# A linear-attention layer and a gated MLP on one Trainium2 core: one vector loaded by transfers, setup work on other engines, and a new table of zero matmuls

## The chip, the cores and the metric

The kernel runs on one core of a Trainium2 chip. The metric is device time in microseconds (us) of one execution; lower is better. Three runs of the kernel before gave 355.48, 359.37 and 359.94 us, median 359.37.

## What is computed

Inputs are float32. `r, k, v, w` are 4 x 8 x 768 x 48 (batch, head, token, channel); `u` is 8 x 48. The attention keeps a 48 x 48 state per head, and its output, laid out as 768 tokens of 384 channels, goes through a gated MLP that mixes along the tokens:

```python
for t in range(S):
    cur = np.einsum('bhd,bhe->bhde', u[None] * kt, vt)
    y[:, :, t] = np.einsum('bhd,bhde->bhe', rt, state + cur)
    state = wt[:, :, :, None] * state + np.einsum('bhd,bhe->bhde', kt, vt)
...
h = np.maximum(x @ w_in, 0.0)                       # 384 -> 1024
u, v = (h[..., :d_ff // 2], h[..., d_ff // 2:])
v_n = (v - mu) / np.sqrt(var + 1e-06)
v_s = np.einsum('ts,bsd->btd', w_spatial, v_n) + b_spatial[None, :, None]
gated = u * v_s
return (gated @ w_out).astype(np.float32)           # 512 -> 384
```

## The kernel before, in words

The work is cut into 24 slots (`NS`): 4 batches of 6 chunks of 128 tokens. A slot of the attention goes like this. `slot_load` fetches the decays `W`, the pair `kr` (k and r by channel) and `v`. `slot_prep` multiplies pairs of decays into `W2p`, scans them forward and back into `E` and `F`, and scales k and r with these. `slot_a` forms the 64 x 64 score tiles in PSUM (`paw`), and VectorE copies their lower half into a tile `AS` (two such tiles in turn, which must hold zeros elsewhere). `slot_kt` transposes k (`pt`, copied to `KT`), `slot_d` multiplies `KT` with `v` into `paw`, `slot_s` and `slot_w` carry the state `S0`, `S1`. `slot_y` and `slot_inter` accumulate the outputs in two PSUM banks, `PY[0]` and `PY[1]` (`py`), and `slot_x` adds the banks into `y`, transposes it (`yt`) and splits it into a high and a low part `xT`.

In the first six slots (`B_PE`) the term with `u` is a matmul: `rk` = r times k, then `pg` = `rk` times `up_sb`, where `up_sb` holds `u` by channel, one column per head (`bonus`, L445). VectorE multiplies `pg` with `v` into `bv`, and a matmul with the identity adds that to `PY[0]` (L597). `up_sb` is made in the kernel: `u_sb[:1]` is loaded as one row, eight matmuls (`spread`, L1112) turn it into columns in PSUM (`pu_`), and two copies (L1118) bring them to `up_sb`. Later slots multiply with the full `u_sb` and use `id64`, two 64 x 64 pieces of the identity.

The MLP follows slot by slot: `hv_unit` (`ph`), the mean and variance (`scale`), then per batch `g_unit` (`pu` for the gate, `pv` for the mix along the tokens) and `out_unit` (`po`, copied to `ot` and stored). Products of float32 are three fp32r matmuls of high and low parts (`mm3`, L714 to L716). The weights are fetched as raw 64-bit words and split by `split64`; the parts are called `wv`, `wu` and `wo`. `check_w` loads each decay tensor once more (`Nw`, L426) and tests it on ScalarE (L427); `Nw` shares one buffer with `N`.

The order of everything is written out by hand. Each operation is recorded with the engines that it may run on, and the table `PLAN` gives for each the engine (T for TensorE, V VectorE, A ScalarE, G GpSimd, S for SyncE, which issues the loads) and a start time; `plan` sorts by start, and each engine executes its operations in that order, waiting on semaphores. `place` gives tiles their buffers in the same order; the tag `pm` has three PSUM banks that `pg`, `pt`, `yt`, `ph`, `pu`, `pv` and `po` share.

Between real matmuls the kernel issues zero matmuls (`warm`, L1070): a 128 x 128 tile of zeros times itself, added to an unused part of the bank `PY[0]`. `fill` decides how many stand ahead of each TensorE operation: it walks through the planned times, and where it finds a gap of over 0.3 us, it puts in as many zeros as the gap should hold. It stops at the operation `last`, after slot 5. The first zeros wait for the clearing of `PY[0]` on VectorE.

The setup ahead of all that clears `zk`, `zz` and both banks `PY` on VectorE (L292 to L309), makes the identity on GpSimd, and copies `id64` (L326) and `mask` (L345) on VectorE. The two `AS` tiles are cleared in slots 0 and 1 by operations of the plan (L515), here on VectorE. `out_unit` stores a tile of 128 rows in one transfer, or in two where the condition with `SPLIT` holds (five tiles of batch 0).

Of the kernel before, what the change touches and what calls it, by code (L numbers as in the profile page):

```python
# [36 lines left out]
V47l A5e4 V5i8 S3o9 A3vo V4pz V4q2 V5cw A5k6 V5q2 S4gg V4jg V52c V52f V53t A5cy V5cz S4k4 V4xs V52e V52q V53u A5hd
V5ip T1xn T2eh T2gj A2ig A2ks A2lg Shm Swh Syv Gx6 T10u Vq1 V12b V139 Vqr Vsz Vt1 V13u G13y V1aw A1av A13x Vdv V16m
T1ax V1nv A175 T17h A19o T1js T1pc T1cb V1f0 A1fw V1tj T1tg A1ur V1ws T21r A23m T2b5 A2bs T2ii T2kd T2ma A2yd A2ye
A2z2 S1ca S1az S1dx V1c8 T1fy V1dw G1nu G1ez V1fz G1hq V1ik V1k8 G1nw V1th A1yy A1n3 V1iz T1vu V23n A1wf T1ny A1pa  # L40
T1zt T282 T1us V21t A21u V2ke T29g A2bv V2eg T2o8 A2p2 T2ry A2tr T2y8 T30j T32c A377 A378 A379 A3bl V39a V3iq G3t6
G3y9 G41y G41z V47o V4jf A4ji V4rz V4aj A4gi V4py A47p A4gj V5hc S1j1 S1j0 S2bz G2c1 T2c3 V2bw V2c5 G2q6 V2c4 V2d1
V2ef V2q7 G2p4 V2q8 A2gi A2yq V2ee T2st V3db A2nd T2p5 A2q4 T2q5 T3ha T2u5 V30i A3dc V3ei T3io A3lm V3m0 T3o7 A3vl
T3vm A40g T41w T45k T47h A4ag A4dx A4f5 S2yc S2ih S2y9 V2u6 T2vo V30f V39g V3fy V349 V3a4 V3ay V3d2 G3f7 G3oy A396
A3p0 V30h T3qv V3tk A3ph T3fz A3ip T3sn T3wf T3jz V3su A3vp V3we T3xs A47m V47q T49e V4dw T4fl A4gc T4k7 T4ma T4q4
A4ry A4xr A52b S3f8 S34b S3oa V35q T3li V3lj V3p1 V3oz V3lk V3o8 V3q6 V3qu G3qy G3tl A49g V40h V3vk T3z2 V4ah A47i
T3ul A3z4 T4a9 T4ch T40f V4ai G4cj T4dv V4ge V4gf T4jl V4o8 T4p4 A4pv T4s0 T4tx T4vt A4z8 A507 A52g A58b V570 V58g
V59y G5be G5dg V5e3 G5ha A5iq A5ju V5ol A5k7 A5k8 V5tz A5ln A5lo V5v2 T7x9 S3qx A41x S4ci A4dy S4jh A4xc S55k A5ec
T34a T35r T3bk A3ej T5n3 T5ok T5ri T5uh T5xc T5yt V60a V6lw A6oe V6z4 T376 T38n T3ow A3sw T5h9 T5it T5lp T5sy T60b
T61r V637 V6ge A6rs V6up T3a6 T3d1 T3ek A3gj T638 T665 T67l T692 T6aj T6bz V6ey V6fz A6xn V70k T443 T4gk T4hy A4je  # L50
T5ed T5fs T5k9 T5q1 T5vw T64o V6c5 G6t9 A7e9 G7ea T7lk T7n0 T7oh T80p A826 Sa8o T7fp T7h6 T7im T7k3 V7q3 S854 T7z8
T827 T83m T855 A86k Sdct T4xu T4z7 T5bf A5fu T6dg T6ex T6ha T6iz T6ur T6xm V70c G8cq A8kr G8lu T53v T55j T572 A5e5
T6kh T6nd T6ru T6t8 T6w7 T6z2 V7ct G7k7 A7wp V7wq T58h T59x T5cv A5is T7xm T86r T881 T89h T8ay T8cf V8hs G8ht A8j9
# [64 lines left out]
Tqnl Tqp1 Tqqh Tqry Aqtf Sqve Tqdb Tqj6 Tqkn Tqm3 Aqnk Sqtg Vof3 Tqth Vqua  # L118
"""

GAP, FILL_TO, COLD = 0.3, 5, 7.0

EARLY = 8

W3 = 5

KR, AB = 3, 2

SPLIT, PE_END = 5, 10

B_PE = 6

Q = 32
T = D - Q

# [1092 lines left out]
```

## Time and profile before

| | |
|---|---|
| median of three runs | 359.37 us (355.48 to 359.94) |
| the profiled execution | 357.4 us, of which the span from first to last instruction is 355.6 us |
| TensorE busy | 347.8 us, 98% |
| VectorE, ScalarE, GpSimd busy | 280.0, 223.8, 141.8 us |
| TensorE clock granted | 1.000 over the span |
| moved by DMA | 50.17 MB, 23,274 packets |

Busy time counts instructions from start to end; on TensorE neighbours overlap, and the zero matmuls count as busy too. One zero matmul is two rows of the trace, since a float32 matmul runs in two passes. Idle time of an engine is listed with what ended it. In a timeline a row merges equal instructions that follow each other: start, length from the first start to the last end, engine, line, operation, tiles, and count.

### The profile page before, as it was taken

What the parts mean: (1) busy time and instruction counts of PE and PEld (TensorE: products, weight loads), DVE (VectorE), ACT (ScalarE), POOL (GpSimd) and SP (SyncE); (2) the same over time, 40 slices, a digit from 0 to 9 for tenths busy, and PEclk for the clock granted to TensorE, in tenths of its full rate; (3) what the DMA queues carried; (4) which work ended last, traced back from release to release, by engine and by line L of the source; (5) the groups of instructions that cost most, each with busy time, mean ns of one, the idle gap of its engine ahead of it and who ended that gap; (6) DMA issues with size and microseconds to landing.
All of it is one profiled execution on the core that took longest, in us unless ns stands there. A gap on an engine that the chain in (4) does not pass through costs nothing.

```text
span 355.6 us, 11441 instructions
## 1 busy us (share of the span) xinstructions
PE 347.8 (98%) x4644; PEld 324.2 (91%) x4644; DVE 280.0 (79%) x626; ACT 223.8 (63%) x622; POOL 141.8 (40%) x187
## 2 busy tenths in 40 slices
PE   7999999989999999999999999999999999999998
PEld 6878887889999898799999999999999999899997
DVE  8988989898998856989787889676776486589750
ACT  2667989885646688896457646844163768464331
POOL 1242264013165436443546633753525217313630
DMA  7898548963256575653545545335020354230003
GB/s 217 229 269 253 173 145 250 257 192 111 72 150 182 148 205 173 190 142 98 156 133 169 162 147 169 101 111 166 23 90 25 98 182 115 64 113 0 24 25 113
DMA packets 23274, 50.17 MB, mean 141 GB/s; under 512 B 2737, under 2 KB 12082, under 8 KB 23218
## 3 DMA queue, kind: packets, MB, share of 16 engines
q1 hardware_dynamic: 23074, 49.21, 47.2%
q8 instruction: 37, 0.61, 0.8%
q14 instruction: 19, 0.16, 0.2%
q10 hardware_dynamic: 144, 0.20, 0.1%
HBM read 44.67 MB, written 4.72 MB: 139 GB/s over the span
## 4 chain that ended last, share of the span: by engine, by line
PE 82%; DMA 9%; DVE 4%; ACT 3%; issue 2%; POOL 0%; SPq 0%; DVEq 0%; POOLq 0%; ACTq 0%
PE pv L714 7%; PE pv L716 7%; PE pv L715 7%; PE py L587 5%; DMA Nw<-in_gt_dram 5%; PE po L714 4%; PE po L715 4%; PE po L716 4%; PE ph L714 4%; PE pu L714 4%; PE pu L716 4%; PE ph L716 4%; PE pu L715 4%; PE ph L715 4%; PE py L1070 3%; PE paw L551 3%
## 5 line engine op out<-in xcount | busy, mean ns | idle before, releaser
L714 PE MATMUL pv<-ws,vh 128*128 128x384 f32 x144 | 49.5, 344 | 1.1 <-ACT us L955 1.1
L716 PE MATMUL pv<-ws,vl 128*128 128x384 f32 x144 | 48.6, 338 | 0.0
L715 PE MATMUL pv<-ws,vh 128*128 128x384 f32 x144 | 48.5, 337 | 0.0
L714 PE MATMUL pu<-xT,wi 128*128 128x384 f32 x96 | 33.1, 345 | 0.3 <-ACT ot L983 0.3
L714 PE MATMUL po<-wo,gh 128*128 128x384 f32 x96 | 32.9, 343 | 0.0
L716 PE MATMUL pu<-xT,wi 128*128 128x384 f32 x96 | 32.3, 337 | 0.0
L716 PE MATMUL po<-wo,gl 128*128 128x384 f32 x96 | 32.3, 336 | 0.0
L715 PE MATMUL po<-wo,gh 128*128 128x384 f32 x96 | 32.3, 336 | 0.0
L715 PE MATMUL pu<-xT,wi 128*128 128x384 f32 x96 | 32.2, 336 | 0.0
L669 ACT ACTIVATE S<-S,prod 112x48 f32<-112x48 f32 x104 | 26.2, 324 | 5.8 <-DVE S L658 5.4
L714 PE MATMUL ph<-wi,xT 128*128 128x512 f32 x72 | 29.3, 407 | 0.0
L714 PEld LDWEIGHTS pv<-ws,vh 128*128 128x128 f32 x144 | 27.0, 188 | 1.7 <-ACT us L955 1.4
L716 PE MATMUL ph<-wi,xT 128*128 128x512 f32 x72 | 28.3, 393 | 0.0
L715 PE MATMUL ph<-wi,xT 128*128 128x512 f32 x72 | 28.2, 391 | 0.0
L715 PEld LDWEIGHTS pv<-ws,vh 128*128 128x128 f32 x144 | 27.1, 188 | 0.2
L716 PEld LDWEIGHTS pv<-ws,vl 128*128 128x128 f32 x144 | 27.0, 188 | 0.0
L495 POOL TENSOR_TENSOR N<-N,u_sb 128x384 f32<-128x384 f32 x11 | 11.8, 1072 | 30.8 <-DVE N L493 30.5
L482 POOL TENSOR_TENSOR kr<-kr,F 112x496 f32<-112x496 f32 x13 | 14.2, 1094 | 20.3 <-DVE prod L477 4.8
L983 ACT COPY ot<-po 128x384 f32<-128x384 f32 x21 | 9.9, 478 | 18.9 <-PE po L716 17.1
L968 ACT CAST gh<-t 128x384 fp32r<-128x384 f32 x24 | 12.0, 509 | 13.9 <-POOL t L966 7.1
L427 ACT ACTIVATE Nw<-Nw,few 128x768 f32<-128x768 f32 x16 | 15.0, 937 | 8.4 <-DMA Nw<-in_gt_dram 6.9
L714 PEld LDWEIGHTS pu<-xT,wi 128*128 128x128 f32 x96 | 18.0, 188 | 1.5 <-ACT ot L983 0.7
(264 smaller groups left out, 1063.2 us busy)
## 6 DMA issues: line engine op xcount, KB each, us to landing
kr<-in_tr_dram SPq DMA_DIRECT2D x24, 448.0 KB, 4.9
N<-in_nat_dram SPq DMA_DIRECT2D x18, 384.0 KB, 3.3
Nw<-in_gt_dram SPq DMA_DIRECT2D x16, 384.0 KB, 3.5
W<-in_tr_dram SPq DMA_DIRECT2D x24, 225.8 KB, 4.4
v<-in_nat_dram SPq DMA_DIRECT2D x24, 192.0 KB, 4.3
out_dram<-ot SPq DMA_DIRECT2D x18, 192.0 KB, 2.5
wst<-in_w_spT_dram SPq DMA_DIRECT2D x12, 192.0 KB, 4.2
a<-in_w_spT_dram SPq DMA_DIRECT2D x12, 192.0 KB, 2.5
```

The costliest lines, as they stand in the source:

```text
L427: op({"A": 0.95}, lambda: nc.scalar.activation(flat(), flat(), AF.Relu, bias=neg, accum_out=over[:, n:n + 1]), r=[(w, 0)], w=[(w, 0), ("ov ...
L482: op({"V": 0.68, "G": 1.07}, lambda e: e.tensor_tensor(seg(kr()[:R, 0])[:, :, :L2 - 1], seg(kr()[:R, 0])[:, :, :L2 - 1], F()[:, :, 1:].uns ...
L495: lambda e: e.tensor_tensor(N()[:, 0], N()[:, 0], u_sb, ALU.mult), r=[("u", 0)], w=[(N, 0)], port=True)
L551: nc.tensor.matmul(pa()[ks, j, g * L:(g + 1) * L], kr()[rs, 0, ts_], kr()[rs, 1, ts_], start=True, stop=True)
L587: nc.tensor.matmul(py()[row][L * a:L * (a + 1), D * n:D * (n + 1)], x, z, start=(a, row) not in started, stop=not left[0], skip_group_chec ...
L669: e.mul(S1[i % 2][a][:, g, :], S0[:, g, :], Wc[:, g:g + 1])
L714: nc.tensor.matmul(ps, ah, bh, start=first, stop=False, **skip)
L715: nc.tensor.matmul(ps, ah, bl, start=False, stop=False, **skip)
L716: nc.tensor.matmul(ps, al, bh, start=False, stop=last, **skip)
L968: op({"A": act(HT)}, lambda: nc.scalar.copy(gh(), t1()), r=[(t1, 0)], w=[(gh, 0)])
L983: lambda e: (e.copy if e is nc.scalar else e.tensor_copy)(ot(), po()[:, :DM]), r=[(po, 0)], w=[(ot, 0)])
L1070: nc.tensor.matmul(pw, zk, zk, start=False, stop=True, skip_group_check=True)
```

## The change

`up_sb` is now filled by two transfers that gather 48 x 4 single numbers each from an input that holds `u` by channel; the load of one row, the eight matmuls and the two copies are gone. Both `AS` tiles are cleared in the setup, next to `PY[0]`; `PY[1]` is cleared by a ScalarE copy of zeros (only the 384 columns in use), and `id64` is copied by ScalarE. Zero matmuls are no longer counted from planned times: the table `ZEROS` says by an operation's place in the order (in base 36) how many stand ahead of it. `SPLIT` now counts over batches, so eight tiles instead of five are stored in halves. The plan's numbers are now places in the order; the order of the recorded operations that both kernels have is the same on every engine. Code for `LOW_T` and `SUM_T` is added, and both are off.

```diff
 PLAN = """
-Thn Shl Tmk Aou Aoy S1uu S5q3 Shj Ahk Vp0 Vsf Vt0 Au2 V10v S1hr A1lx V1ti V1ut V1wg A21s V2bt S13w A16n V17g V1ay V1uv
+Te Sb Sc S2x Scl S9 Aa Vi Vo Vq Av V16 S24 A2g V2s V2w V31 A37 V3i S1c A1i V1k V1q V2y A3d V3r S0 S6 Ss V7 Tk V1 Vf V8
...
-GAP, FILL_TO, COLD = 0.3, 5, 7.0
+ZEROS = """
+e:8 j:9 10:4 15:2 1l:1 1p:3 21:3 2m:2 2q:5 3f:7 bw:10 cy:2
+"""
+
+FILL_TO = 5
...
-SPLIT, PE_END = 5, 10
+SPLIT, PE_END = 8, 10
...
-    for t in PY:
+    for t in (PY[0], *AS):
         nc.vector.memset(t, 0.0)
+    nc.scalar.copy(PY[1][:, :DM].rearrange("p (k c) -> p k c", c=C), zk.unsqueeze(1).broadcast_to([P, KX, C]))
...
-        nc.vector.tensor_copy(id64[hs], ident[hs, hs])
+        nc.scalar.copy(id64[hs], ident[hs, hs])
...
-            if i < AB:
-                op({"G": 0.5, "V": 0.3}, lambda e: e.memset(As(), 0.0), w=[(As, 0), (As, 1)], port=True)
...
-        cuts = 2 if dst is None and b == 0 and h * NH + j < SPLIT else 1
+        cuts = 2 if dst is None and (b * 2 + h) * NH + j < SPLIT else 1
...
     def fill(order):
-        t = free = 2.3
-        for o in order:
-            if o in held and o.on != "T":
-                free = o.start + o.eng[o.on] + 0.25
-            if o.on == "T":
-                b = max(t, free)
-                if t < last.start and o.start - b > GAP:
-                    cold = max(0.0, min(o.start, COLD) - b)
-                    warm(cold / 0.43 + max(0.0, o.start - max(b, COLD) - 0.1) / 0.224)
-                t = max(t, o.start + o.eng["T"])
+        zeros = {int(n, 36): int(k) for n, k in (w.split(":") for w in ZEROS.split())}
+        for n, o in enumerate(order):
+            if n in zeros:
+                warm(zeros[n])
             yield o
...
-    op({"S": 0.45}, lambda: nc.sync.dma_start(u_sb[:1], u_rep[:1]), w=[("u1", 0)], dma=0.01)
-    pu_ = buf(psM, [P, 512], "pm", "pu_", 3)
-
-    def spread():
-        for j in range(2):
-            for g in range(G):
-                n = 2 * g + j
-                nc.tensor.matmul(pu_()[64 * j:64 * j + D, g:g + 1], u_sb[:1, n * D:(n + 1) * D], ones[:1],
-                                 start=True, stop=True)
-
-    op({"T": 0.6}, spread, r=[("u1", 0)], w=[(pu_, 0)], mode="128x64")
     for j in range(2):
         rs = slice(64 * j, 64 * j + D)
-        op({"A": 0.16, "V": 0.14}, lambda e, j=j, rs=rs: (e.copy if e is nc.scalar else e.tensor_copy)(
-            up_sb[rs, :, j], pu_()[rs, :G]), r=[(pu_, 0)], w=[("up", j)])
+        op({"S": 0.45}, lambda j=j, rs=rs: nc.sync.dma_start(up_sb[rs, :, j], gu[:G, rs, 0].rearrange("g p -> p g")),
+           w=[("up", j)], dma=0.01)
```

The start of VectorE, before. `py` are the two banks, `AS` the score tiles, `id` is `id64`, and `F` and `prod` belong to slot 0.

```order
L292 MEMSET zk 128x128
L297 MEMSET zz 128x512
L309 MEMSET py_88 128x512
L309 MEMSET py_89 128x512
L515 MEMSET AS_85 128x512
L326 COPY id_105<-ident 64x64 x2
L298 MEMSET zz 128x8
L345 CAST mask<-mneg 64x64 x2
L468 TENSOR_TENSOR W2p<-W_141 112x256
L475 SCALAR_TENSOR_TENSOR F_144<-zz,W2p 112x256
L515 MEMSET AS_86 128x512
L477 TENSOR_SCALAR prod<-F_144 112x8
```

And with the change:

```order
L286 MEMSET zk 128x128
L291 MEMSET zz 128x512
L303 MEMSET py_88 128x512
L303 MEMSET AS_85 128x512
L303 MEMSET AS_86 128x512
L292 MEMSET zz 128x8
L340 CAST mask<-mneg 64x64 x2
L471 TENSOR_TENSOR W2p<-W_142 112x256
L478 SCALAR_TENSOR_TENSOR F_145<-zz,W2p 112x256
L480 TENSOR_SCALAR prod<-F_145 112x8
```

One clearing of a bank and the two copies left the setup, and the second score tile's clearing moved there from behind the first scan. From here on both kernels have the same VectorE instructions.

TensorE in slot 2, before: the last matmuls ahead of the products of the score tile with `v` and `vs`.

```order
L716 MATMUL ph_0_513<-wi_122,xT_0_1_416 128x512
L597 MATMUL py_88<-bv_400,ident 128x384
L697 MATMUL yt_519<-ident,y_470 128x128 x3
L1070 MATMUL py_88<-zk 128x128 x8
L587 MATMUL py_88<-v_372,AS_85 64x48
L587 MATMUL py_89<-v_372,AS_85 64x48
```

With the change the zeros stand behind the 16 products with the score tile, ahead of those with the state `S`:

```order
L588 MATMUL py_88<-v_368,AS_85 64x48
L588 MATMUL py_89<-v_368,AS_85 64x48
L588 MATMUL py_89<-vs_411,AS_85 64x48
L588 MATMUL py_88<-vs_411,AS_85 64x48
L1084 MATMUL py_88<-zk 128x128 x7
L588 MATMUL py_88<-S_117,kr_343 64x48
L588 MATMUL py_89<-S_117,kr_343 64x48
```

Eight zeros became seven and moved behind the products that don't need the state.

TensorE in the first `g_unit`s of batch 0, before: two products of `pv_0_3`, then the first of `pv_0_1`.

```order
L716 MATMUL pv_0_3_1306<-ws_124,vl_0_1178 128x384
L714 MATMUL pv_0_3_1306<-ws_124,vh_1_1115 128x384
L715 MATMUL pv_0_3_1306<-ws_125,vh_1_1115 128x384
L716 MATMUL pv_0_3_1306<-ws_124,vl_1_1165 128x384
L714 MATMUL pv_0_1_1316<-ws_124,vh_0_1133 128x384
L715 MATMUL pv_0_1_1316<-ws_125,vh_0_1133 128x384
```

With the change ten zeros stand between them, where there were none:

```order
L730 MATMUL pv_0_3_1304<-ws_126,vl_0_1176 128x384
L728 MATMUL pv_0_3_1304<-ws_126,vh_1_1113 128x384
L729 MATMUL pv_0_3_1304<-ws_127,vh_1_1113 128x384
L730 MATMUL pv_0_3_1304<-ws_126,vl_1_1163 128x384
L1084 MATMUL py_88<-zk 128x128 x10
L728 MATMUL pv_0_1_1324<-ws_126,vh_0_1131 128x384
L729 MATMUL pv_0_1_1324<-ws_127,vh_0_1131 128x384
```

Ten matmul groups further on, two more zeros stand ahead of a product of `pv_0_3`. The other counts, in the order of the program, before and now: at the start 15 and then `spread`, now 18; ahead of `bv` of slot 0 three, now four; ahead of `pg` of slot 1 none, now two; ahead of `pg` of slot 2 two, now three; ahead of the state's products of slot 1 three, now five; the places not named here have the same count. In all 38 zeros before the last ten of the program became 58.

## Rows read from the trace of the kernel before

**Rows 1.** The page: busy time by engine, and shares of the chain by engine.
```profile
PE 347.8 (98%) x4644; PEld 324.2 (91%) x4644; DVE 280.0 (79%) x626; ACT 223.8 (63%) x622; POOL 141.8 (40%) x187
...
PE 82%; DMA 9%; DVE 4%; ACT 3%; issue 2%; POOL 0%; SPq 0%; DVEq 0%; POOLq 0%; ACTq 0%
```

**Rows 2.** Waits of PE: line, what for: us in total, times, longest.
```profile
PE pv L714 <- ACT us L955: 1.1, 1, 1.1
PE pt L570 <- issue: 0.8, 1, 0.8
...
PE yt L697 <- DVE zz L479: 0.4, 1, 0.4
```

**Rows 3.** Timeline of all engines, 0 to 13 us.
```profile
0.89 1.28 ACT L317 ACT_TABLE_LOAD   x1 [0.89 <-PEq L1217]
...
1.80 1.02 DVE L309 MEMSET py<- 128x512 f32 x2
...
2.31 0.33 SPq L1105 DMA_DIRECT2D u_sb<-in_u_rep_dram  x1
...
2.68 0.32 SPq L412 DMA_DIRECT2D W<-in_tr_dram  x1
2.92 0.48 DVE L515 MEMSET AS<- 128x512 f32 x1
...
3.32 0.33 DVE L326 COPY id<-ident 64x64 f32<-64x64 f32 x2
...
4.16 0.43 DVE L468 TENSOR_TENSOR W2p<-W 112x256 f32<-112x256 f32 x1
...
5.37 0.48 DVE L515 MEMSET AS<- 128x512 f32 x1
...
5.77 0.11 DVE L477 TENSOR_SCALAR prod<-F 112x8 f32<-112x8 f32 x1
...
7.99 0.72 PE L1112 MATMUL pu__180<-few,u_sb 1*48 1x1 f32 x16
...
8.22 0.68 ACT L380 ACTIVATE e_('wv', 0)_158<-d_('wv', 0)_156 128x512 f32<-128x512 f32 x1 [5.64 <-DMA d_('wv', 0)_156<-in_w_in_dram]
...
9.33 0.42 DVE L382 TENSOR_SCALAR e_('wv', 0)_158<-e_('wv', 0)_158 128x512 int32<-128x512 int32 x1
...
9.51 0.57 PE L570 MATMUL pt<-ident,kr 112*128 112x112 f32 x4 [0.81 <-issue]
...
9.67 0.42 DVE L468 TENSOR_TENSOR W2p<-W 112x256 f32<-112x256 f32 x1
```

**Rows 4.** DMA: first and second `W` (us to landing last), queues in 0:30, whole span.
```profile
W<-in_tr_dram SPq DMA_DIRECT2D x1, 225.8 KB, 2.6
...
W<-in_tr_dram SPq DMA_DIRECT2D x1, 225.8 KB, 6.6
...
q1 hardware_dynamic: 2788, 7.10, 86.2%
...
q10 hardware_dynamic: 144, 0.20, 0.1%
```

**Rows 5.** Timeline of PE, then of ACT, 22 to 30 us.
```profile
22.97 0.94 PE L1070 MATMUL py<-zk 128*128 128x128 f32 x6
...
27.60 1.95 PE L1070 MATMUL py<-zk 128*128 128x128 f32 x16
29.48 0.26 PE L587 MATMUL py<-v,AS 64*64 64x48 f32 x2
...
27.30 1.01 ACT L669 ACTIVATE S<-S,prod 112x48 f32<-112x48 f32 x4
```

**Rows 6.** Timeline of PE, then of ACT, 72 to 74 us.
```profile
72.31 0.34 PE L716 MATMUL pv<-ws,vl 128*128 128x384 f32 x1
73.78 0.44 PE L714 MATMUL pv<-ws,vh 128*128 128x384 f32 x1 [1.12 <-ACT us L955]
...
72.32 0.94 ACT L427 ACTIVATE Nw<-Nw,few 128x768 f32<-128x768 f32 x1 [1.26 <-DMA Nw<-in_gt_dram]
```

More of the change, by code (lines that the diff above doesn't have):

```diff
@@ L37 @@
[L37 to L41, printed above, removed]
@@ new lines @@
+Vcw Th5 S79 A81 S8s A8x S9h Aac Saz Abq T5i T5l T60 A68 Tcg Tch Tcm Tcv Td0 Td4 Vd5 Ve9 Aec Vf4 T5m T5q T6x A7e Tbw
+Tc7 Tcf Tcp Td6 Td7 Vd8 Vdz Aem Ves T5w T63 T69 A6g Td9 Tdb Tdd Tde Tdf Tdi Vdt Vdu Af0 Vf7 T86 T9b T9c A9e Tbr Tbs
+Tcc Tcj Tcy Tda Vdo Geq Afx Gfy Tg9 Tgg Tgh Thc Ahd Smh Tfz Tg0 Tg1 Tg2 Vgo Shk Tha The Thf Thl Ahm Stk Tag Tai Tbc
+Abu Tdp Tds Te2 Te3 Teu Tez Vf5 Gi2 Ail Gio Tax Tay Tb4 Abo Te6 Teb Teo Tep Tex Tf2 Vfu Gg6 Ah3 Vh4 Tb8 Tb9 Tbe Ac6
+Th9 Tht Thu Thw Thx Thz Vic Gid Aie Gip Tea Teg Tej Aey Tf8 Tfa Tfq Tfr Tfs Tfw Vg5 Ggk Ahg Vhp Tj6 Tja Tjb Tjp Ak2
@@ L385, in split64 @@
         op({"A": act(n)}, lambda: nc.scalar.copy(hi, parts()[2].bitcast(F32)), r=[(em, 0)], w=[(*key, 0)])
+        if key in LOW_T:
+            pl = buf(psM, [P, 512], "pm", f"pl_{key}", 3)
+            op({"T": 0.88}, lambda: nc.tensor.matmul(pl()[:, :n], ident, parts()[2].bitcast(F32), start=True, stop=False),
+               r=[(em, 0)], w=[(pl, 0)])
+            op({"T": 0.23}, lambda: nc.tensor.matmul(pl()[:, :n], nident, hi, start=False, stop=True),
+               r=[(*key, 0)], w=[(pl, 0)])
+            op({"A": act(n, True), "V": dve(n)},
+               lambda e: (e.copy if e is nc.scalar else e.tensor_copy)(lo, pl()[:, :n]), r=[(pl, 0)], w=[(*key, 1)])
+            return
         op({"G": pool(n), "V": dve(n)},
@@ L400 @@
     st = [dict() for _ in range(NS)]
-    held = set()
     def slot_load(i):
@@ L698, in tp, with more @@
                                  stop=k_ == KX - 1, is_transpose=True, skip_group_check=True)
+        def more():
+            for k_ in range(KX):
+                nc.tensor.matmul(yT()[:, k_, :], y1()[:, k_ * P:(k_ + 1) * P], ident, start=False,
+                                 stop=k_ == KX - 1, skip_group_check=True)
         op({"T": 0.245}, tp, r=[(y, 0)], w=[(yt, 0)])
+        if i < SUM_T:
+            op({"T": 0.64}, more, r=[(y1, 0)], w=[(yt, 0)])
         op({"A": 0.48, "V": 0.55}, lambda e: (e.copy if e is nc.scalar else e.tensor_copy)(hi()[:, :, cs], yT()),
@@ L1149 @@
         if i == FILL_TO:
-            prog.last = last = op({"T": 0.1}, lambda: warm(1), r=[(vn[0, c][0], 0)], w=[("pw", 0)])
+            op({"T": 0.1}, lambda: warm(1), r=[(vn[0, c][0], 0)], w=[("pw", 0)])
         if c == NC_ - 1:
```

167 lines of the change are left out of this document (81 added, 86 removed).

## The prediction, made before the run

> **What bounds the kernel now.** I read the page's busy times and its chain first. TensorE (PE) is busy for 98% of the span, and PE makes up 82% of the chain that ended last [rows 1]. Little idle time is left to take out, so I read PE's waits next: the only ones that this change comes near are 0.8 us ahead of the first transpose, 0.4 us ahead of a transpose of `y`, and 1.1 us in the middle of a `pv` [rows 2]. But "busy" includes the zero matmuls. So the third view is the timeline around each run of zeros, to see whether the matmul behind them could have started earlier.
>
> The reader is to see three stretches. Up to about 10 us VectorE works without a pause from its setup into slot 0, PE waits for it, and the loads come in one behind the other: the second `W`, of the same size as the first, was issued at 2.68 us and took 6.6 us to land, where the first took 2.6 [rows 3, 4]. From there to 30 us PE and VectorE hand work to each other. Then PE is full, apart from the one hole at 72 us, which ends with a load that ScalarE waits for [rows 6].
>
> **The change part by part.** I take sums against the profiled execution, 357.4 us (span 355.6 and 1.8 around it). It lies 2 us below the median, 359.37, and inside the three runs, which are themselves 4.5 us apart.
>
> *VectorE's setup.* The two bank clearings take 1.02 us, so one is 0.51; the `id64` copies go (0.33); one score tile's clearing, 0.48, is added there: 0.51 + 0.33 - 0.48 = 0.36 us earlier for the first `W2p`, 3.80 instead of 4.16. Its `W` was issued at 0.92 and needed 2.6, so it is there at 3.5 [rows 3, 4]. The second clearing leaves the gap between scan and `prod`: from 5.37 to 5.77 that is another 0.40. VectorE is then 0.76 us ahead at the scaling of k and r, and PE's first transpose, at 9.51, can come at 8.75. PE gets there no earlier: `spread` ended at 8.71, and the three extra zeros in its place, at 0.235 us each (sixteen rows, that is eight zeros, from 27.60 to 29.48 [rows 5]), end at 7.99 + 0.70 = 8.69.
>
> The lead does not last. VectorE's L382 needs ScalarE's conversion of `wv 0`, which starts when the load lands, at 8.22, and ends at 8.90 [rows 3]; so L382 comes at about 8.95 instead of 9.33, 0.38 earlier. Behind it stands the `W2p` of slot 1, at 9.67, and its `W` landed at 2.68 + 6.6 = 9.28. So VectorE gains at most 0.38 us, just as much as that load allows.
>
> *The transfers of `u`.* This is the cost that no row of before shows. Two gathers of 192 numbers are 384 packets of 4 bytes, 24 on each of the 16 engines, in place of one row of 1.5 KB. They stand behind the first `W`, `kr` and `wv 0` and ahead of the second `W`, both `v` and all further loads, in a queue that is 86.2% busy up to 30 us. On SyncE one issue of 0.33 becomes two; the loads behind are in a backlog of several microseconds, so that hides. In the queue, the price of a packet is bounded from below by its bytes, which is nothing, and from above by a mean packet up to 30 us: 0.862 x 30 x 16 / 2788 = 0.148 us, for 2.5 KB, or 24 x 0.148 = 3.6 us. The shortest packets of the trace are those of queue 10: 0.001 x 355.6 x 16 / 144 = 0.04 us for 1.4 KB, which makes 0.95 us [rows 4]. As a packet of 4 bytes carries next to nothing, I take half of that, 0.5 us, for the lateness of all loads behind. VectorE at slot 1 then stands at -0.38 + 0.5 = +0.1 us.
>
> A rule that speaks against this edit: the Trainium skill, "DMA: Bandwidth & Descriptors", section "Rules for kernel authors", says that a transfer whose last dimension is not contiguous becomes one descriptor per number. Its section "Measured" gives some 10.5 ns a packet; by that 384 would take 4.0 us, an estimate close to my upper bound, and the sum would be that of the second rival. No row here shows such packets.
>
> `up_sb` itself is first read by `pg`, behind the transpose, and would land soon after `wv 0`, so near 8.7; `pg` begins after 9.
>
> *ScalarE.* It gets one more table load (1.28) and three copies, each shorter than that load, so under 5.1 us. It now sits idle for 5.64 us until `wv 0` lands [rows 3]. That hides all of it; without the cover it would delay L382 one for one. `id64` is not read before slot 6.
>
> *Zeros up to 31 us.* Four and two zeros around slot 0's `bv` against three: three more, 0.7 us, in the 0.76 that PE is ahead there. I take nothing; with the cover gone they cost 0.7. One more ahead of slot 2's `pg` falls into the 0.4 us wait behind it [rows 2]: nothing. Five for three ahead of slot 1's state products: PE runs straight on there (six rows at 22.97), and the state's parts are old. I see no cover: 2 x 0.235 = +0.47. In slot 2, eight become seven and move behind the score products. The state that the next products need is ready at 27.30 + 1.01 = 28.3; before, PE went through zeros until 29.48, so PE set the pace, and it does again. One zero less: -0.24 [rows 5].
>
> *Zeros at 72 us.* PE's hole of 1.12 us ends when ScalarE has done `Nw`, whose load landed at 72.3, and then the gate that frees a PSUM bank [rows 6]. Ten zeros take 2.35 us. If the hole is as long as here, they run over by 2.35 - 1.12 = 1.2 us. If the load lands 1.2 us later, they cost nothing. This hangs on a landing, and the runs spread more than that; I take the middle, 0.6. The two zeros some five microseconds later stand where PE has no wait: +0.47. Later waits of PE are short and follow PE itself through buffers and loads, so I let all of this reach the end.
>
> *Stores.* Three more tiles go out in halves: three more issues of some 0.33 us on SyncE [rows 3], far apart and ahead of loads that have their own waits. Nothing, or 1 us if each delayed a load that PE waits for.
>
> The sum: 0.1 + 0.47 - 0.24 + 0.6 + 0.47 = +1.4 us, so 358.8.
>
> **The rivals.**
>
> *The zeros sit in waits, and the small packets are nearly free.* For it: bytes weigh nothing, the hole at 72 us is set by a load whose landing can move, and a hole at slot 1 may open when PE is early. Against it: PE shows no wait at two of the places. Then only -0.38 and -0.24 remain: 356.8 us.
>
> *The small packets hold up the load queue (the slower side).* Place: the queue, between `wv 0` and the second `W`. Price: at 0.148 us a packet, 3.6 us; it decides from the point where the second `W` lands after 9.67, that is from 0.4 us of delay on. VectorE then waits 9.28 + 3.6 - 9.67 = 3.2 us in place of a gain, and the rest of the sum (1.3) stays: 357.4 + 3.2 + 1.3 = 361.9. For it: the queue is full just there and packets go one behind the other. Against it: the shortest packets seen cost a quarter of that.
>
> *The zeros don't do what they are for.* If fewer zeros stood where PE must wait long, its clock could fall. The granted clock is 1.000 all through before, 2.4 GHz of the two levels, beside waits of 0.8 and 1.1 us; now there are more zeros, so I give it little. To lose 2% it would need some 15 us at half speed.
>
> **How the numbers follow.** Forecast (357.5 to 360.5) 0.5; the first rival 0.3; the second 0.17; anything else 0.03. The range goes from below the first rival, with the runs' own spread, to the second: 355.2 to 362.2. A difference of 2%, 7.2 us, is about what a measurement of this kernel can tell from no change. All cases lie within it: 0.95 for the same, 0.02 faster (no term can gain 7 us), 0.03 slower.
>
> **What would show it.** The trace after should have some 380 more packets under 512 B; the second `W` landing at 9.7 to 9.9; PE's first transpose at 8.7 to 8.8; slot 1's `W2p` within 0.4 us of 9.67; zeros directly followed by matmuls, with no idle time ahead, where I gave them a price; and no idle time left at 72 us. I am wrong if the second `W` lands at 9.3 or after 11, if PE still waits behind the ten zeros, or if the end moves by more than 4 us.

## The result, and the profile after

| | before | after |
|---|---|---|
| median | 357.5 us (354.51 to 362.18, 21 runs; the three shown ahead are among them) | 359.46 us (357.79 to 365.76, 21 runs) |
| ratio after to before | | 1.009, 95% interval 1.007 to 1.0109 |
| the profiled execution | 357.4 us, span 355.6 | 358.73 us, span 357.0 |

The change makes the kernel slower by about 3.2 us (0.009 x 357.5): well within 2%, but the interval lies clear of 1. Runs that were disturbed are left out of the ratios. The page after, for [rows 1], and the waits of PE, for [rows 2]:

```profile
PE 350.7 (98%) x4668; PEld 328.0 (92%) x4668; DVE 277.7 (78%) x623; ACT 226.0 (63%) x624; POOL 141.6 (40%) x187
...
PE 91%; ACT 4%; DVE 2%; DMA 1%; issue 1%; POOL 0%; DVEq 0%
```

```profile
PE paw L644 <- issue: 0.8, 1, 0.8
PE py L1084 <- DVE py L602: 0.7, 1, 0.7
```

PE's share of the chain rose from 82 to 91%, and its busy time by 2.9 us. The wait behind which a `pv` stood, 1.1 us for ScalarE, is no longer in the list. A wait of a zero matmul (`py L1084`) for VectorE's L602 has come in its place. The next view is the timeline of the first 13 us, for [rows 3], lines of several engines in order of time; the one after it is the DMA view for [rows 4] (the second `W`, then both transfers of `u`, then the whole span).

```profile
2.31 0.92 SPq L1115 DMA_DIRECT2D up_sb<-in_gu_dram  x2
3.27 0.44 SPq L415 DMA_DIRECT2D W<-in_tr_dram  x1
3.82 0.43 DVE L471 TENSOR_TENSOR W2p<-W 112x256 f32<-112x256 f32 x1
7.58 0.68 ACT L375 ACTIVATE e_('wv', 0)_158<-d_('wv', 0)_156 128x512 f32<-128x512 f32 x1 [2.71 <-DMA d_('wv', 0)_156<-in_w_in_dram]
8.81 0.57 PE L571 MATMUL pt<-ident,kr 112*128 112x112 f32 x4 [0.54 <-issue]
8.96 0.42 DVE L471 TENSOR_TENSOR W2p<-W 112x256 f32<-112x256 f32 x1
```

```profile
W<-in_tr_dram SPq DMA_DIRECT2D x1, 225.8 KB, 5.7
...
up_sb<-in_gu_dram SPq DMA_DIRECT2D x2, 0.8 KB, 5.5
...
DMA packets 23736, 50.17 MB, mean 141 GB/s; under 512 B 3200, under 2 KB 12544, under 8 KB 23680
```

The front came out ahead. The first `W2p` starts at 3.82, 0.34 earlier; ScalarE still sits idle for 2.71 us ahead of `wv 0`, so its added work is hidden; the first transpose comes at 8.81 instead of 9.51; and the second `W` landed at 3.27 + 5.7 = 8.97, before the 9.28 of the kernel before and outside the 9.7 to 9.9 that I had named. Slot 1's `W2p` starts 0.71 us earlier.

The lead is lost between 22 and 26 us: the run of zeros ahead of slot 1's state products starts at 22.67, 0.30 earlier than before, and is four rows longer, and behind it PE waits 0.53 us for nothing that the profile shows, where before it waited 0.20. PE, for [rows 5], and then PE, VectorE and ScalarE round the ten zeros, for [rows 6]:

```profile
22.67 1.38 PE L1084 MATMUL py<-zk 128*128 128x128 f32 x10
...
25.05 0.38 PE L588 MATMUL py<-S,kr 48*64 48x48 f32 x11 [0.53 <-issue]
...
28.78 1.83 PE L1084 MATMUL py<-zk 128*128 128x128 f32 x14
...
72.68 0.34 PE L730 MATMUL pv<-ws,vl 128*128 128x384 f32 x1
73.25 0.38 DVE L602 MEMSET py<- 128x384 f32 x1
73.28 0.47 ACT L969 ACTIVATE us<-pu 128x384 f32<-128x384 f32 x1
73.69 2.50 PE L1084 MATMUL py<-zk 128*128 128x128 f32 x20 [0.67 <-DVE py L602]
75.94 0.42 PE L728 MATMUL pv<-ws,vh 128*128 128x384 f32 x1
...
81.10 0.34 PE L730 MATMUL pv<-ws,vl 128*128 128x384 f32 x1
81.28 0.61 PE L1084 MATMUL py<-zk 128*128 128x128 f32 x4
81.64 0.42 PE L728 MATMUL pv<-ws,vh 128*128 128x384 f32 x1
```

This is the place. The gate copy (`us`, ScalarE) that frees the bank for the next `pv` ends at 73.75; in before, the `pv` that waits for it started at 73.78 [rows 6]. But the ten zeros stand ahead of that `pv`, and they did not start when PE came free: they write into `PY[0]`, and VectorE clears the other columns of `PY[0]` for slot 6 just then (L602, 73.25 to 73.63). So PE waits through the hole, and the zeros, meant for it, follow it. The `pv` starts at 75.94, where before it started at 73.78. The chain of waits says the same: it runs through VectorE's clearing and then through all ten zeros (start, length, what).

```profile
73.25 0.39 DVE py L602
...
73.69 2.50 PE py L1084 x20
```

Matched instruction by instruction, PE after stands 0.35 us behind PE before at 56 us (after's start less before's), 2.16 at 74, 2.51 at 79 and 1.57 at 141. Then the wait of 0.77 us for `y` that before has at 144 us (first line) is absent, which leaves 0.64; and a stall near 186 us (second line), 0.76 us of idle time and 1.0 by the starts, puts it at 1.69.

```profile
144.24 0.55 PE L697 MATMUL yt<-ident,y 128*128 128x128 f32 x3 [0.77 <-DVE y L693]
...
186.77 0.38 PE L644 MATMUL paw<-v,KT 64*48 64x48 f32 x12 [0.76 <-issue]
```

### The profile page after: what moved, and what is told of

It reads as the page before. It is cut to its first block, busy times and chain, and to the rows that moved or that the text cites. A ratio compares the mean times of both kernels' runs of the same rounds, so it can differ in the third digit from the quotient of the medians.

```text
span 357.0 us, 11492 instructions
## 1 busy us (share of the span) xinstructions
PE 350.7 (98%) x4668; PEld 328.0 (92%) x4668; DVE 277.7 (78%) x623; ACT 226.0 (63%) x624; POOL 141.6 (40%) x187
## 4 chain that ended last, share of the span: by engine, by line
PE 91%; ACT 4%; DVE 2%; DMA 1%; issue 1%; POOL 0%; DVEq 0%
PE pv L728 7%; PE pv L730 7%; PE pv L729 7%; PE py L588 6%; PE py L1084 5%; PE po L728 5%; PE po L729 5%; PE po L730 5%; PE ph L728 4%; PE pu L728 4%; PE pu L730 4%; PE ph L730 4%; PE pu L729 4%; PE ph L729 4%; PE paw L552 3%; PE paw L644 3%
## 5 line engine op out<-in xcount | busy, mean ns | idle before, releaser
L1084 PE MATMUL py<-zk 128*128 128x128 f32 x136 | 19.8, 298 | 3.2 <-DVE py L303 2.3
L1084 PEld LDWEIGHTS py<-zk 128*128 128x128 f32 x136 | 18.1, 208 | 4.2 <-DVE py L303 2.3
L980 POOL TENSOR_TENSOR t<-t,us 128x384 f32<-128x384 f32 x13 | 13.7, 1054 | 17.3 <-DVE t L978 12.8
```

What stands on the lines that cost most here:

```text
L980: op({"V": dve(HT), "G": pool(HT)}, lambda e: e.tensor_tensor(t1(), t1(), us(), ALU.mult), r=[(us, 0)], w=[(t1, 0)], port=True)
L1084: nc.tensor.matmul(pw, zk, zk, start=False, stop=True, skip_group_check=True)
```

## The experiments

There were three groups, e1 to e4, e5 to e8 and e9 to e12. Each ran beside the kernel before in five rounds, the first two on one chip, the third on another. Between groups the ratios are compared, since the median of before itself moves by over 1 us. "Clock 1.000" counts the runs that list that mean granted clock.

| kernel | median us | ratio to before (95%) | clock 1.000 |
|---|---|---|---|
| before, in the three groups of runs | 357.12, 355.99, 357.19 | | 14 of 29, 14 of 24, 16 of 35 |
| after | 359.46 | 1.009 (1.007 to 1.0109) | 20 of 21 |
| e1 no late zeros | 355.78 | 0.9978 (0.9947 to 1.0009) | 12 of 12 |
| e2 late zeros tiny | 357.47 | 1.0027 (0.9988 to 1.0066) | 11 of 12 |
| e3 old zeros | 359.61 | 1.0043 (0.9999 to 1.0088) | 2 of 12 |
| e4 new zeros, old front | 362.72 | 1.0161 (1.0111 to 1.0212) | 2 of 6 |
| e5 slot 0's counts back | 357.65 | 1.0074 (1.0042 to 1.0106) | 3 of 7 |
| e6 three for five | 355.75 | 0.9966 (0.9935 to 0.9997) | 11 of 12 |
| e7 move undone | 355.91 | 1.0005 (0.9974 to 1.0036) | 11 of 12 |
| e8 zeros in the other bank | 358.82 | 1.009 (1.0057 to 1.0124) | 6 of 6 |
| e9 four times the packets | 356.81 | 0.9988 (0.9952 to 1.0024) | 11 of 12 |
| e10 setup undone | 357.15 | 1.0007 (0.9974 to 1.0039) | 11 of 12 |
| e11 new early zeros, old front | 358.0 | 1.0027 (0.9988 to 1.0066) | 10 of 12 |
| e12 four late zeros | 356.49 | 0.9984 (0.995 to 1.0018) | 11 of 12 |

### The twelve late zeros

e1 takes them out of the changed kernel.

```diff
-e:8 j:9 10:4 15:2 1l:1 1p:3 21:3 2m:2 2q:5 3f:7 bw:10 cy:2
+e:8 j:9 10:4 15:2 1l:1 1p:3 21:3 2m:2 2q:5 3f:7
```

> The changed kernel without the ten and the two zeros of 72 and 81 us. Theory: these cost 2.2 us at 72 and 0.4 at 79 us of TensorE's time, of which waits up to 145 us give back 1.9, and the 1.05 us stall at 185 us hangs on where TensorE's instructions stand, so that it can go too: the end comes 0.5 to 1.7 us earlier than the changed kernel's, ratio to before 1.001 to 1.006. Rival (the loss comes from the front and the loads): ratio stays at 1.009.

The ratio fell from 1.009 to 0.9978; the intervals do not touch. Twelve zeros of 128x128 cost 1.1%, some 4 us, more than everything else in the change together, and more than my theory had left for them. e1's profiled execution is the slowest of its twelve (358.80 us), so I read it for the place only. At 72 us the hole is there again, and its end is the gate copy, as in [rows 6]:

```profile
73.00 0.34 PE L730 MATMUL pv<-ws,vl 128*128 128x384 f32 x1
73.65 0.47 ACT L969 ACTIVATE us<-pu 128x384 f32<-128x384 f32 x1
74.17 0.45 PE L728 MATMUL pv<-ws,vh 128*128 128x384 f32 x1 [0.83 <-ACT us L969]
```

Here 1.17 us lie between the two starts of PE, in the changed kernel 75.94 - 72.68 = 3.26. A second reading needs only one execution: the `pv` follows the end of the gate copy by 0.05 us here, by 0.06 in before, and by 75.94 - 73.75 = 2.19 in the changed kernel. By both the ten zeros cost 2.1 us at this place. The gate copy in before:

```profile
73.25 0.47 ACT L955 ACTIVATE us<-pu 128x384 f32<-128x384 f32 x1
```

The two later ones cost 81.64 - 81.10 = 0.54 less the 0.18 at which neighbours follow each other, 0.36.

e2 keeps all twelve, as the same number of instructions in the same places, but with a product of 16 x 16 numbers.

```diff
+    def tiny(us):
+        for _ in range(int(us)):
+            nc.tensor.matmul(pw[:16, :16], zk[:, :16], zk[:, :16], start=False, stop=True, skip_group_check=True)
...
-                warm(zeros[n])
+                (tiny if n > 400 else warm)(zeros[n])
```

> The changed kernel with the same twelve late zero matmuls, but 16 x 16 instead of 128 x 128: as many TensorE instructions as the changed kernel, almost none of the time. Theory: they still wait for the clearing of the bank at 72 us, but the pv behind starts at 73.8 to 74.3 instead of 75.9; the stall at 185 us stays, if it hangs on the number of instructions ahead. Ratio to before 1.004 to 1.008. Rival (the stall is a late load): no stall at that matmul.

```profile
74.47 0.67 PE L1088 MATMUL py<-zk 128*16 128x16 f32 x20 [1.12 <-DVE py L602]
74.53 0.47 ACT L969 ACTIVATE us<-pu 128x384 f32<-128x384 f32 x1
75.06 0.44 PE L728 MATMUL pv<-ws,vh 128*128 128x384 f32 x1
...
186.03 0.38 PE L644 MATMUL paw<-v,KT 64*48 64x48 f32 x12 [0.89 <-issue]
```

About half of the price goes with the size of the zeros (1.0027 lies between 0.9978 and 1.009, and below the range that I expected). The wait for L602 stays, here 1.12 us, but with tiny zeros behind it this wait costs nothing: the gate copy ends at 75.00, and the `pv` follows at 75.06. What the rows still show as a loss is mainly a stall near 186 us, of which more below.

e8 writes all zeros into the free columns of `PY[1]`, which nobody clears at 73 us.

```diff
-    pw = PY[0][:, DM:]
+    pw = PY[1][:, DM:]
...
-    nc.scalar.copy(PY[1][:, :DM].rearrange("p (k c) -> p k c", c=C), zk.unsqueeze(1).broadcast_to([P, KX, C]))
+    nc.scalar.copy(PY[1].rearrange("p (k c) -> p k c", c=C), zk.unsqueeze(1).broadcast_to([P, KX + 1, C]))
```

> The changed kernel with all its zeros, written into the unused columns of PY[1] instead of PY[0] (ScalarE's copy in the setup clears all 512 columns of it). Theory W (the ten late zeros wait for VectorE's clearing of PY[0], and that wait is about 1 us of their price): in the profile they start as soon as PE is free, near 72.7 us, the pv behind them at 74.9 to 75.1 instead of 75.94, and the median is 0.8 to 1 us below the changed kernel's, a ratio near 1.006. Theory N (the count alone is the price; the wait costs nothing, as PE would have waited then anyway): the pv at 75.9 as before, ratio 1.009.

```profile
72.79 0.34 PE L730 MATMUL pv<-ws,vl 128*128 128x384 f32 x1
72.97 2.39 PE L1084 MATMUL py<-zk 128*128 128x128 f32 x20
73.91 0.47 ACT L969 ACTIVATE us<-pu 128x384 f32<-128x384 f32 x1
75.12 0.42 PE L728 MATMUL pv<-ws,vh 128*128 128x384 f32 x1
...
186.04 0.38 PE L644 MATMUL paw<-v,KT 64*48 64x48 f32 x11 [0.87 <-issue]
```

The wait is gone: the zeros start as soon as PE is free, and from the last `pv` ahead to the first behind it is 75.12 - 72.79 = 2.33 us, 0.93 less than in the changed kernel and 1.16 more than in e1. So the profile splits the 2.1 us: 0.9 is the wait for the clearing, 1.2 the zeros that a hole as short as e1's does not hold. In e8's own execution the gate copy ended later, at 74.38, and the `pv` followed it by 0.74, so there only 0.7 us ran over. The medians do not show the 0.9: 358.82 against 359.46 is in the right direction, but the two ratios are both 1.009 with intervals of some 0.3% to either side. In time, the wait alone stays unproven.

e12 puts four zeros into the hole, in `PY[1]`, and none later.

```diff
-e:8 j:9 10:4 15:2 1l:1 1p:3 21:3 2m:2 2q:5 3f:7 bw:10 cy:2
+e:8 j:9 10:4 15:2 1l:1 1p:3 21:3 2m:2 2q:5 3f:7 bw:4
```

> The changed kernel with four instead of ten zeros ahead of the pv at 72 us, written into PY[1], and none ahead of the pv after it. Theory F (zeros that fit into the hole of about 1 us cost nothing): the pv starts at the same time as in the version without late zeros, and the median is within 0.5 us of 355.8. Theory G (the hole closes by itself when PE is later, so that every zero there costs its time): 4 x 0.25 = 1.0 us more, 356.8 or above.

```profile
73.47 0.34 PE L730 MATMUL pv<-ws,vl 128*128 128x384 f32 x1
73.64 1.05 PE L1084 MATMUL py<-zk 128*128 128x128 f32 x8
74.70 0.47 ACT L969 ACTIVATE us<-pu 128x384 f32<-128x384 f32 x1
75.22 0.44 PE L728 MATMUL pv<-ws,vh 128*128 128x384 f32 x1 [0.53 <-ACT us L969]
```

Four zeros leave an idle 0.53 us behind them, and the `pv` follows the gate copy by 0.05 us, as in e1, so they fit. The two starts of PE are 1.75 us apart, 0.58 more than in e1, because the gate copy came later. The median is 0.7 us above e1's, on another chip, and the ratio 0.0006 higher. That is between the two expectations in time, while the rows side with the first. The end of the hole is no fixed time: in profiles without any late zeros PE's wait there was 0.83 us (e1), 0.99 (e6), 0.53 (e7), 1.6 (e10) and none that the list of waits shows (e9). So I can say that four are nearly free and ten are not.

### The early zeros

e3 gives the changed kernel the counts and places of the zeros of before.

```diff
-e:8 j:9 10:4 15:2 1l:1 1p:3 21:3 2m:2 2q:5 3f:7 bw:10 cy:2
+e:8 j:6 10:3 1l:1 1p:3 21:2 2m:2 2q:3 3e:8
```

> The changed kernel with the zeros in the places and counts of the kernel before (15 at the start, 38 in all). Theory: the front keeps 0.3 to 0.7 us of its lead to 31 us, and the end comes 0 to 0.7 us ahead of before: ratio 0.998 to 1.000. Rival (the transfers of u or the clearing cost): ratio 1.003 or more.

It has no late zeros and is still 3.8 us slower than e1 in the median, and only 2 of 12 runs list a clock of 1.000. The number, 1.0043, is that of the rival, but its cause is not: e1 has the same transfers and clearing and stands at 0.9978. e3's profiled execution shows such a run: PE's timeline, and then the windows (in each: length, then busy time of PE, its weight loads, VectorE, ScalarE and GpSimd with counts, the granted clock, the DMA share and GB/s).

```profile
27.34 0.60 PE L644 MATMUL paw<-v,KT 64*48 64x48 f32 x27 [2.64 <-issue]
...
28.75 0.79 PE L728 MATMUL ph<-wi,xT 128*128 128x512 f32 x1
```

```profile
24.00:26.00 2.00, 0.70 (x36) 0.58 (x37) 1.35 (x3) 1.35 (x5) 1.05 (x1) 1.00 1.04 345
26.00:28.00 2.00, 0.66 (x41) 0.66 (x44) 0.00 (x0) 1.00 (x3) 0.22 (x1) 0.93 0.97 259
28.00:30.00 2.00, 2.00 (x34) 1.69 (x28) 1.03 (x3) 0.64 (x3) 0.00 (x0) 0.50 0.45 122
```

PE stood still for 2.64 us, waiting for nothing that the profile shows. Behind that the granted clock was 0.50 over 28 to 30 us (1.2 GHz, the lower of the two levels), and a `ph` matmul, 0.50 us in the changed kernel, took 0.79. The stall and the clock together set this execution back.

Which zeros matter was asked with three single steps back from e1. e5 takes back the start's and slot 0's counts and slot 2's one zero (seven zeros: three, three and one), e6 the five ahead of slot 1's state products, e7 the move in slot 2.

```diff
-e:8 j:9 10:4 15:2 1l:1 1p:3 21:3 2m:2 2q:5 3f:7
+e:8 j:6 10:3 1l:1 1p:3 21:2 2m:2 2q:5 3f:7
```

```diff
-e:8 j:9 10:4 15:2 1l:1 1p:3 21:3 2m:2 2q:5 3f:7
+e:8 j:9 10:4 15:2 1l:1 1p:3 21:3 2m:2 2q:3 3f:7
```

```diff
-e:8 j:9 10:4 15:2 1l:1 1p:3 21:3 2m:2 2q:5 3f:7
+e:8 j:9 10:4 15:2 1l:1 1p:3 21:3 2m:2 2q:5 3e:8
```

> The changed kernel without the twelve late zeros, and with the counts around slot 0 as before (6 and 3 instead of 9, 4 and 2, and 2 instead of 3 ahead of slot 2's pg). Theory A (each zero matmul costs its 0.235 us unless PE would wait): these seven zeros hold nothing back, so at most 1 us faster than the version without the late zeros (355.8), 354.8 to 355.8. Theory B (the zeros of slots 0 to 2 decide how often PE has a long idle time or its clock falls in the first 35 us): these zeros are the ones that matter, so the times spread again from 355 to 361 with a median near that of the version with all the old zeros, 359.6.

> The changed kernel without the late zeros, with three zeros instead of five ahead of slot 1's state products. Theory A: 0.47 us less, 355.3. Theory B, if these two zeros are the ones that matter: a median of 358 or more and a spread of 5 us; if not, 355.3 to 355.8 in a narrow band.

> The changed kernel without the late zeros, with eight zeros ahead of slot 2's score products instead of seven behind them. Theory A: 0.24 us more, 356.0. Theory B, if the place of these zeros is what matters: 358 or more, a spread of 5 us, and in the profile a long idle time of PE or a lower granted clock between 24 and 32 us.

e5 alone brings a loss: 1.0074, and 3 of 7 runs at 1.000. e6 and e7 stay at 11 of 12 and at e1's median within 0.2 us, so neither the two zeros at slot 1 nor the move has a price that these runs can tell. The seven zeros of e5 hold some 1.6 us of PE's time (7 x 0.235) and are worth 0.5% by the medians and 0.7 to 1.1% by the ratios of e6 and e7 beside them; which of the seven matter was not asked. The same split runs through all versions that load `u` by transfers: with the new counts there 104 of 111 runs list 1.000 (after, e1, e2, e6 to e10, e12), with the old ones 5 of 19 (e3, e5), and the kernel before 44 of 88. What that is worth shows in before: its 44 runs at 1.000 have a median of 355.8 us, the others 358.6. e1, all at 1.000, has 355.8 too, so against before at the same clock it gains nothing that these runs can tell. How the zeros do it was not seen in rows: the profiled execution of e5 had a clock of 1.000 and none of its waits longer than 0.35 us behind the first zeros.

e4 puts the new table on the kernel before (the same twelve places, on its own front); e11 is e4 without the late zeros.

```diff
     def fill(order):
-        t = free = 2.3
...
+        zeros = {15: 9, 18: 5, 40: 4, 45: 2, 61: 1, 65: 3, 77: 3, 98: 2, 102: 5, 127: 7, 432: 10, 470: 2}
+        for n, o in enumerate(order):
+            if n in zeros:
+                warm(zeros[n])
```

```diff
-        zeros = {15: 9, 18: 5, 40: 4, 45: 2, 61: 1, 65: 3, 77: 3, 98: 2, 102: 5, 127: 7, 432: 10, 470: 2}
+        zeros = {15: 9, 18: 5, 40: 4, 45: 2, 61: 1, 65: 3, 77: 3, 98: 2, 102: 5, 127: 7}
```

> The kernel before with the new table's zeros at the same TensorE operations, and nothing else of the change (15 zeros and the column matmuls at the start as before). Theory: the zeros carry the whole loss and no lead of the front pays for part of it: ratio 1.009 to 1.012. Rival: 1.000 to 1.004.

> The kernel before with the new counts of zeros up to slot 2 and none of the late ones. Theory A (the twelve late zeros cost 3.5 us wherever they are put): 359.2, that is 3.5 less than with them on this front (362.7). Theory C (what made that kernel slow was the early zeros in front of a VectorE that is 0.7 us later): still over 361.

e4 came out above both of its expectations. From 1.0161 to 1.0027: on this front too the late zeros cost 1.3%, and the same wait stands ahead of the ten (e4's timeline of PE):

```profile
76.23 2.50 PE L1070 MATMUL py<-zk 128*128 128x128 f32 x20 [1.11 <-DVE py L601]
```

e11 fell further than the 3.5 us that its first theory named (4.7 in the medians) and is still above e1 (1.0027 against 0.9978), though the intervals overlap, so whether the new counts suit the new front better than the old one is not shown. Why e4 ran at a lower clock in 4 of 6 runs where e11 did in 2 of 12 is open, and it is not the price: e4's two runs at 1.000 took 362.3 and 362.4 us. In e4's profile the clock fell to 0.50 over 12 to 14 us, with PE busy throughout:

```profile
10.00:12.00 2.00, 2.00 (x71) 1.99 (x72) 1.97 (x5) 0.88 (x2) 0.00 (x0) 0.91 1.05 280
12.00:14.00 2.00, 2.00 (x19) 1.88 (x15) 2.00 (x6) 1.63 (x5) 1.27 (x1) 0.50 1.05 273
```

### The front

e9 and e10 are steps from e1, without the late zeros. e9 gathers 48 x 16 numbers per transfer instead of 48 x 4; only the first four of each row are used.

```diff
-    up_sb = cp.tile([R, G, 2], F32, name="up_sb")
+    b_sb = cp.tile([P, S], F32, name="b_sb")
+    up_sb = b_sb[:R, :2 * B * G].rearrange("p (g j) -> p g j", j=2)
     nc.gpsimd.memset(up_sb, 0.0)
-    b_sb = cp.tile([P, S], F32, name="b_sb")
...
-        op({"S": 0.45}, lambda j=j, rs=rs: nc.sync.dma_start(up_sb[rs, :, j], gu[:G, rs, 0].rearrange("g p -> p g")),
+        op({"S": 0.45}, lambda j=j, rs=rs: nc.sync.dma_start(up_sb[rs, :, j], gu[:, rs, 0].rearrange("g p -> p g")),
```

> The version without the late zeros, in which the two transfers of u gather 48 x 16 numbers instead of 48 x 4 (1,536 packets of 4 bytes instead of 384, with the same two issues; they go into a part of b_sb, which is loaded much later). Theory S (a packet of 4 bytes is next to free in the queue): the second W lands within 0.5 us of the 8.97 us of the changed kernel, slot 1's first product on VectorE starts before 9.5, and the median is within 1 us of 355.8. Theory Q (each small packet holds the queue for some 0.04 us): 72 more on each of the 16 engines delay the second W by about 2.9 us, to 11.8, and with it slot 1: 358 to 359.

```profile
3.35 0.70 SPq L415 DMA_DIRECT2D W<-in_tr_dram  x1
...
W<-in_tr_dram SPq DMA_DIRECT2D x1, 225.8 KB, 6.6
...
9.99 0.43 DVE L471 TENSOR_TENSOR W2p<-W 112x256 f32<-112x256 f32 x1 [0.83 <-DMA W<-in_tr_dram]
```

With 1,152 more small packets the second `W` took 6.6 us to land. In the ten profiled executions with 384 it took 5.7 to 6.8, with a median of 6.05, and the three without took 6.3, 6.6 and 6.7. So 72 more on each engine cost 0.55 us against that median (6.6 - 6.05), some 8 ns each, and 0.9 us against the earliest, some 12 ns each; both are within the scatter, so this is an estimate of the most that they cost. The expectation of 2.9 us falls, and with it my upper bound of 148 ns. The signs of theory S did not all come either: the `W` landed at 9.95 and slot 1's `W2p` started at 9.99, but with 384 packets e10's started at 9.95. The 10.5 ns a packet that the Trainium skill gives ("DMA: Bandwidth & Descriptors", section "Measured", there for transfers issued by GpSimd) would make 12 us of 1,152 packets if they went one behind the other in all, and 0.76 us of 72 on each engine, both estimates. No delay of 12 us is here; one of 0.76 would lie between the two figures above. The prediction read that figure the first way.

The trace before the change already held the price of such packets. Its page counts 2,737 packets under 512 B, and in the trace 2,721 packets on the load queue have 4 bytes, with a recorded length of 9 ns in the median. At that, 24 more on each engine make 0.2 us.

```profile
DMA packets 23274, 50.17 MB, mean 141 GB/s; under 512 B 2737, under 2 KB 12082, under 8 KB 23218
```

e10 undoes the setup: VectorE clears and copies as before.

```diff
-    for t in (PY[0], *AS):
+    for t in (*PY, AS[0]):
...
-    nc.scalar.copy(PY[1][:, :DM].rearrange("p (k c) -> p k c", c=C), zk.unsqueeze(1).broadcast_to([P, KX, C]))
...
-        nc.scalar.copy(id64[hs], ident[hs, hs])
+        nc.vector.tensor_copy(id64[hs], ident[hs, hs])
...
+        def floor(e):
+            if i == 0:
+                nc.vector.memset(AS[1], 0.0)
+            e.tensor_scalar(Wc, F()[:, :, 0], FLOOR, None, ALU.max)
+
+        op({"V": 0.17, "G": 0.24}, floor,
...
```

> The version without the late zeros, with the setup as before: VectorE clears both banks and one score tile, copies the identity pieces, and clears the second score tile between scan and prod. Theory L (the 0.7 us that VectorE gains at slot 1 reach the end): 0.7 us slower, 356.5. Theory H (from 10 us on PE's own work and the zeros set the pace, so the head start is used up): within 0.3 us of 355.8. If the later VectorE makes PE wait longer at slot 0 so that its clock falls, some runs show a mean granted clock of 0.995 or less and the median is 357 or more.

```profile
9.52 0.57 PE L575 MATMUL pt<-ident,kr 112*128 112x112 f32 x4 [0.57 <-issue]
...
9.95 0.43 DVE L470 TENSOR_TENSOR W2p<-W 112x256 f32<-112x256 f32 x1 [0.20 <-DMA W<-in_tr_dram]
```

The first transpose is back at 9.52, as in before, and the median is 1.4 us above e1's, more than either theory gave (1.0007 against 0.9978, on another chip, with intervals that overlap). This speaks for a head start that reaches the end, against one that is used up, but it is not shown, and a size cannot be read from it. The clock stays at 1.000 in 11 of 12 runs, so with the new counts it holds without VectorE's head start.

The three more stores in halves were not tried alone.

## Why the prediction was right or wrong

The forecast was 358.8 and the median is 359.46, inside the range and within 2%. For the profiled execution the sum said +1.4, and it came out 358.73 - 357.4 = +1.3. That the sum fits is luck: its terms are wrong in both directions. Beside the median of many runs before, 357.5, the change costs 3.2 us, more than twice the sum. The three runs shown ahead of the prediction had a median 1.9 us too high, and beside that median the forecast even reads as a small gain, where the kernel became slower. I took the profiled execution for the base without asking how the clock of other executions stood.

**The step that failed: "ten zeros take 2.35 us ... they run over by 2.35 - 1.12 = 1.2 us ... I take the middle, 0.6".** The overrun is right where nothing else holds the zeros: e8 shows 0.7 us in its own, longer hole, and 1.16 against e1's. What I left out is that a zero matmul has an operand that others write. It adds to `PY[0]`, and VectorE's clearing of `PY[0]` for slot 6 ends only when the hole is nearly over. So the zeros came behind the hole: 2.1 us instead of 0.6. I had named "if PE still waits behind the ten zeros" as a sign of error; PE waited ahead of them, 0.67 us. I looked at what ended the hole, and not at what the zeros wait for, though the text ahead of the prediction says that the first zeros wait for the clearing of this bank.

**The two zeros at 79 us, +0.47:** 0.36. Right.

**"Later waits of PE are short ... so I let all of this reach the end."** Right, as far as the rows go, but a term was missing. e7 has none of the late zeros, and its other step, in slot 2, has left no lead by 72 us. Matched instruction by instruction with e7's execution, the changed kernel stands 0.15 us ahead there, 2.23 behind at 74, 2.67 at 83, still 2.67 at 170, and 3.7 from 188 us to the end. What before itself loses between 83 and 145 us is no part of the price: e7 gains the same 2.0 us on it there. Only the wait of 0.8 us for `y` at its end is open, since it comes and goes: before, e1, e6 and e10 have it, and with or without late zeros the other ten do not. The missing term is a stall that was in no row of before: 0.76 us of idle time in the changed kernel, 0.89 in e2, 0.87 in e8, each at the same `paw` near 186 us, and 1.0 to 1.2 us by the matched starts. These are the three kernels on this front with the twelve late instructions; in e1 and e7 the same stretch has no idle time of PE. What makes the stall is not shown.

**Zeros around slot 0: "I take nothing".** This was the other large miss. As time on PE they are indeed hidden. But with the three at the start and the one in slot 2 they are worth 0.5 to 1% (e5): without these seven 4 of 7 runs list a clock below 1.000. My third rival asked whether fewer zeros could lower the clock, and I gave it little because before's profile showed 1.000 throughout. That profile was one execution; half of before's runs (44 of 88 at 1.000) are not like it. So the change has two sides: the early zeros keep the clock up in more executions, and with the front bring the ratio to 0.9978, not clear of 1 (e1); the late zeros take it to 1.009.

**Slot 1's five for three, +0.47, and slot 2, -0.24.** PE runs straight into the five, as I said, but e6 without two of them and e7 with the old place and count differ from e1 by 0.03 and 0.13 us in the median, both inside the intervals.

**The transfers of `u`, +0.5 for the lateness of loads.** Wrong in size: 0.2 us by the recorded lengths, and no more than the scatter of a landing can hide (e9), so the second rival, which needed 3.6 us, falls. "No row here shows such packets" was wrong too, as the page before counts 2,737 under 512 B; the packets of queue 10 were not the shortest. After the change there are 463 more of them, where I had named some 380. The landing that I used as an edge, 9.28, moves by 1.1 us between executions with the same loads, so no plan to 0.4 us could rest on it. The first rival was right in this half and wrong in the other, that the late zeros sit in waits.

**VectorE and ScalarE.** Right: 3.82 for 3.80 and 8.81 for 8.75, and ScalarE's work is covered. `wv 0` landed at 7.58, so the gain at slot 1 was 0.71 and not 0.38 in this execution.

The lowest ratio is e6's: the changed kernel without the late zeros and with three for five, 0.9966 of before (0.9935 to 0.9997). e1 lies beside it, within the noise. Either is faster than the changed kernel by over 1%.

## What to carry to other kernels

A padding matmul is an instruction with operands: before it is put into a hole, look for what last writes its bank or tile and when, or give it a bank that nobody touches there. A hole that ends with another engine's work or a load has another length in each execution (here from none to 1.6 us), so fill less than one profile shows. And judge padding that is there for the clock by the mean granted clock of many executions, not by one profile: here seven zeros, hidden in time, decided 0.5 to 1%.

## What the runs showed of the hardware that I had not expected

- Granted clock: the same program ran at 1.000 in one execution and below it in the next (before: 44 of 88 at 1.000). In e3 the fall came behind 2.64 us in which PE stood still; in e4 it came while PE was busy, for 1.88 of the 2 us from 8 to 10 us and throughout from 10 to 20 us.
- PE stalls that wait for nothing shown: 0.53 us in the changed kernel and 0.69 in e6 at 25 us among slot 1's state products, 2.64 in e3 a little further on, and the one near 186 us, which the three kernels on the new front with all twelve late instructions have, whatever their size (e2), and e1, e7 and e12 do not. The trace has one 16 KB packet of the instruction queue between 183 and 187 us in the changed kernel, but in e1 too, which has no stall there; the cause is open.
- Packets of 4 bytes: a recorded length of 9 ns in the median, and some 8 to 12 ns each on an engine as the most by a landing (e9, one execution).
- The same second `W` landed 5.7 to 6.8 us after its issue in ten executions with the same loads ahead of it.
